# Off-by-one softmax attention and a squared-ReLU feed-forward layer: reordering the opening of a fused kernel, with squares on GpSimd

## The chip, the cores and the metric

The kernel runs on one core of one Trainium2 chip. The metric is device time in microseconds of one execution. A core has TensorE (PE, matrix products, with weight loads shown as PEld), VectorE (DVE), ScalarE (ACT), GpSimd (POOL) and SyncE (SP), which work through their own instruction queues in order and wait for each other by semaphores; data moves between the memory of the device and the core through DMA queues, issued here by SP, ACT and POOL.

## The reference

Inputs are q, k and v of shape (8 batches, 12 heads, 448 positions, 64), and two weights, `w_in` (768 x 2048) and `w_out` (2048 x 768), all float32.

```python
scores = (q @ k.T) / 8
m = max(scores, axis=-1)
e = exp(scores - m)
attn = e / (sum(e) + exp(-m) + 1e-9)
x = (attn @ v), heads put side by side   # (8*448, 768)
h = x @ w_in
out = (max(h, 0) ** 2) @ w_out           # (3584, 768)
```

Multiplying numerator and denominator of `attn` by exp(m) gives exp(scores) / (1 + sum of exp(scores)), up to the 1e-9; the kernel computes this, without the maximum.

## The kernel before

**Tiling.** Two heads form a pair (6 pairs a batch), and a unit is one pair with a stretch of queries. Batch 0 is cut in two by queries: units 0 to 5 are its six pairs with the first 192 queries, units 6 to 11 the same pairs with the last 256. From unit 12 on a unit is one pair with all 448 queries; units 12 to 17 are batch 1, and so on to batch 7. The keys of a unit are taken in 4 chunks of 112, two chunks in each of two *score visits*.

**One unit.** `scores(u, et, c)` is score visit c: TensorE multiplies keys by queries into PSUM (L187 for batches 0 to 2, L199 after) and ScalarE takes the exponential into `et` (L167), one exponential a visit in batch 0 and two from batch 1 on. PSUM has two score buffers. `add_chunks` adds the four chunks of `et` on VectorE (L212, L214 with 448 queries, L216, L219 with fewer), down to a tile `es`. `row_sums` multiplies `es` by a column of ones on TensorE (L248), which sums over partitions, and ScalarE makes the reciprocal as exp(-ln(sum + 1)) (L251, L252, tile `rcp`). `values` multiplies `et` by v on TensorE (L234), and `normalise` multiplies by the reciprocal on VectorE into `xt` (L260, L263), the transposed input of the feed-forward layer.

**The feed-forward layer.** `tile_in` makes one tile of h: TensorE products (called by `product`, L284; in two column halves of 64 that are two matmul instructions, one product), the ReLU on VectorE into `rt` (L301), the square on VectorE into the ring `gs` (L303). A product is one 128-block of `w_in` (16 blocks of 128 columns) with one of six 128-row chunks of `xt`. `tile_out` multiplies `gs` by `w_out` (L330; L286 at the end) and scales into `ot`, which SP stores.

**Order.** There is no scheduler: the order of the instructions on each engine is the order in which this program records them. `queue(t0, n)` puts the `tile_in` tiles of n tokens from t0 into a list, and `drain(ns)` takes products from the list until about `ns` nanoseconds of TensorE work are recorded. Hand-set shares of that work fill TensorE between the attention steps. `run` takes whole tiles.

- Batch 0 and the first queries are transposed by TensorE: `cast` makes float16 (L146 on ScalarE for the first k, L148 on VectorE), `transposes` turns (L156) and VectorE copies to `qk` (L162). Batches 1 and 2 go the same way from float16 loads (`load_natural`). From batch 3 on the DMA transposes (`stage`, `transposed_loads`).
- `keep_warm` records matmuls on zeros that nobody reads, to keep TensorE running in the opening.
- The first loop (`for i in range(2 * NPAIR)`) is batch 0. At unit 6 the list gets the first projection of the first 192 tokens, and units 7 to 11 drain it.
- The second loop is batch 1. In each unit: score visit 0, transposes, drain, score visit 1, row sums and values of the unit before, drain, the adds of this unit, the normalise of the unit before. Row sums of unit i-1 come after score visit 1 of unit i.
- After that comes a loop over pairs of units from batch 2 on (`rows` drains `tile_out`). In its first block the list's leftovers run, and the row sums and values of unit 17 are done.
- Tiles in PSUM come from pools: two score buffers (`s_psum`), three buffers `mp` for transposes, feed-forward tiles, row sums and warm matmuls, and one `xp` for values. A tile that needs a buffer waits until the engine that reads the older one has finished with it.
- GpSimd (POOL) issues the loads that convert to float16, in the order of the program.

Of the kernel before, what the change touches and what calls it, by code (L numbers as in the profile page):

```python
# [15 lines left out]
def kernel(  # L16
# [9 lines left out]
    nc = tc.nc  # L26

    B, H, S, D = q.shape
# [22 lines left out]
    e_pool = ctx.enter_context(tc.tile_pool(name="e", bufs=4))  # L51
    es_pool = ctx.enter_context(tc.tile_pool(name="es", bufs=2))
    z_pool = ctx.enter_context(tc.tile_pool(name="z", bufs=2))
    r_pool = ctx.enter_context(tc.tile_pool(name="r", bufs=2))
    osb_pool = ctx.enter_context(tc.tile_pool(name="osb", bufs=2))

    s_psum = ctx.enter_context(tc.tile_pool(name="s_psum", bufs=2, space=bass.MemoryType.PSUM))
# [19 lines left out]
    def load_v(b, p0, p1):  # L77
        hs = slice(2 * p0, 2 * p1)
        if b not in vns:
            vns[b] = v_pool.tile([P, H, RUN, D], FP16, name="vn")  # L80
        nc.gpsimd.dma_start(out=vns[b][:, hs], in_=v_r[b, :, hs])

    def load_natural(b, p0, p1):

        raw = b == 0 and p1 <= 3
        for n, r in (("q", q_r), ("k", k_r)):
            src = r[b, :, 2 * p0:2 * p1]
            if raw:
                if p0 == 0:
                    whole[n] = e_pool.tile([P, RUN * S], FP32, name="et")  # L90
                t = whole[n][:, p0 * 512:(p0 + 1) * 512].rearrange("p (h t d) -> p h t d", h=2, t=RUN)
                (nc.sync if n == "q" else nc.scalar).dma_start(out=t, in_=src)
            else:
                if p0 % 3 == 0:
                    whole[n] = nat.tile([P, NPAIR, RUN, D], FP16, name=f"{n}n{p0 // 3}")
                t = whole[n][:, 2 * (p0 % 3):2 * (p0 % 3 + p1 - p0)]
                nc.gpsimd.dma_start(out=t, in_=src)
            for pr in range(p0, p1):
                naturals[n, b, pr] = t[:, 2 * (pr - p0):2 * (pr - p0) + 2]
# [42 lines left out]
    def cast(b, pr):  # L142
        for name in "qk":
            f = flat.tile([P, 2, RUN, D], FP16, name=f"flat{name}")
            if b == 0 and pr == 0 and name == "k":
                nc.scalar.activation(out=f, in_=naturals[name, b, pr], func=AF.Copy)  # L146
            else:
                nc.vector.tensor_copy(f, naturals[name, b, pr])  # L148
            naturals[name, b, pr] = f

    def transposes(b, pr):
        tp = mp_tile(FP16)
        for i, name in enumerate("qk"):
            for s in range(RUN):
                for h in range(2):
                    nc.tensor.transpose(tp[64 * h:64 * h + 64, i, P * s:P * s + P],  # L156
                                        naturals[name, b, pr][:, h, s, :], ident[0:P, 0:P])
        if b not in qks:
            qks[b] = qk_pool.tile([128, 3, COLS], FP16, name="qk")
        parts = (0, S // 2, S) if b == 0 and pr == 0 else (0, S)  # L160
        for x, y in zip(parts, parts[1:]):
            nc.vector.tensor_copy(qks[b][:, 0:2, pr * S + x:pr * S + y], tp[:, :, x:y])  # L162

# [111 lines left out]

    FULL, COLS2, ROWS2 = range(3)
    mode = [FULL]
    ots = {}

    def product(out_, lhsT, rhs, start, stop):  # L280
# [7 lines left out]
    def tile_in(t0, n, f0, per):  # L288

        xt, x0 = xts[t0 // S], t0 % S  # L290
        m = per * n
        hp = mp_tile()
        for j in range(per):
            fb = f0 + j
            for dc in range(DCH):
                product(hp[:, j * n:(j + 1) * n], win[:, dc, fb * 128:(fb + 1) * 128],
                        xt[:, dc, x0:x0 + n], start=(dc == 0), stop=(dc == DCH - 1))
                if j < per - 1 or dc < DCH - 1:
                    yield n / 2.4
        rt = r_pool.tile([128, 512], FP16, name="rt")  # L300
        nc.vector.tensor_scalar(out=rt[:, 0:m], in0=hp[:, 0:m], scalar1=0.0, scalar2=None, op0=ALU.max)  # L301
        r = rt[:, 0:m].rearrange("p (j n) -> p j n", j=per)
        nc.vector.tensor_mul(gs[:, f0:f0 + per, t0 % RING:t0 % RING + n], r, r)  # L303
        yield n / 2.4

    def store(c, ot, n0, n1):
# [48 lines left out]
    for pr in range(3):  # L355
        load_natural(0, pr, pr + 1)
    nc.scalar.preload_act_table_set("natural_log_exp_and_others")
    load_v(0, 0, 3)
    ident = consts.tile([128, 128], FP16)
    make_identity(nc, ident)  # L360
    load_natural(0, 3, 4)
    load_natural(0, 4, 6)
    load_v(0, 3, 6)
# [9 lines left out]
    ins, outs = [], []  # L373
    groups = [0]

    def queue(t0, n):

        per = max(1, 512 // n)
        for f0 in range(0, NFFB, per):
            ns = per * DCH * n / 2.4  # L380
            ins.append([ns, ns, tile_in(t0, n, f0, per)])

# [33 lines left out]

    transpose_at = {pr - 1: (0, pr) for pr in range(1, NPAIR)}
    for pr in range(NPAIR):
        transpose_at[NPAIR + 3 + pr] = (1, pr)
    transpose_at[16], transpose_at[17] = (2, 0), (2, 1)  # L420

    def keep_warm(n):
        wp = m_psum.tile([128, 512], FP32, name="mp")
        for _ in range(n):
            nc.tensor.matmul(wp, warm[:, 0:128], warm, start=True, stop=True)
# [18 lines left out]
    keep_warm(9)  # L444
    cast(0, 0)
    transposes(0, 0)
    keep_warm(3)
    cast(0, 1)


    for i in range(2 * NPAIR):
        u, et, es, half = begin(i)
        two = units[i - 2:i] if i and i % 2 == 0 else None
        if i % 2:
            xp = x_psum.tile([128, 512], FP32, name="xp")
        mode[0] = COLS2
        scores(u, et, 0)
        if i == 0:
            keep_warm(4)
        if i == NPAIR:  # L460
            values(units[i - 1], ets.pop(i - 1), xp, units[i - 1][3])
            rcp = row_sums(two, (ess.pop(i - 2)[0:1], ess.pop(i - 1)[0:1]))
            normalise(two, xp, rcp)
            queue(0, FIRST)
            share[0] = left() / (NPAIR + 2)
        if i in transpose_at:
            transposes(*transpose_at[i])
        if i == 0:
            cast(0, 2)
        if i > NPAIR:  # L470
            drain(share[0] * 0.45)
        scores(u, et, 1)
        if 0 < i < NPAIR:
            keep_warm(1)
        if i and i != NPAIR:
            if two and i < NPAIR:
                rcp = row_sums(two, (ess.pop(i - 2)[0:1], ess.pop(i - 1)[0:1]))
            values(units[i - 1], ets.pop(i - 1), xp, (i - 1) % 2 * units[i - 1][3])
            if two and i > NPAIR:
                rcp = row_sums(two, (ess.pop(i - 2)[0:1], ess.pop(i - 1)[0:1]))  # L480
        if i > NPAIR:
            drain(share[0] * 0.3)
        add_chunks(u, et, es, half, 1)
        if two and i != NPAIR:
            normalise(two, xp, rcp)
        add_chunks(u, et, es, half, 2)
        if i > NPAIR:
            drain(share[0] * 0.25)
        if i == NPAIR + 5:
            load_natural(2, 0, 3)  # L490
            for j in range(2):
                load_wout(0, j, 2)


    for i in range(2 * NPAIR, 3 * NPAIR):
        u, et, es, half = begin(i)
        prev = units[i - 1]
        first = i == 2 * NPAIR
        if not first:
            xp = x_psum.tile([128, 512], FP32, name="xp")  # L500
        mode[0] = COLS2
        scores(u, et, 0)
        if i in transpose_at:
            transposes(*transpose_at[i])
        if i == 2 * NPAIR + 2:
            load_natural(2, 3, 6)
            for j in range(2):
                load_wout(HALF, j, 2)
            load_v(2, 0, 6)
            stage(3)  # L510
        drain(left() * 0.5 if first else share[0] * 0.45)
        scores(u, et, 1)
        if first:
            done = units[i - 2:i]
            values(prev, ets.pop(i - 1), xp, prev[3])
            rcp = row_sums(done, (ess.pop(i - 2)[0:1], ess.pop(i - 1)[0:1]))
        else:
            done = [prev]
            rcp = row_sums(done, (ess.pop(i - 1)[0:1],))
            values(prev, ets.pop(i - 1), xp)  # L520
        drain(share[0] * 0.15)
        for step in range(3):
            add_chunks(u, et, es, half, step)
            drain(share[0] * (0.15, 0.1, 0.15)[step])
        if i == 3 * NPAIR - 1 and ins and ins[0][0] < ins[0][1]:
            run(ins)
        normalise(done, xp, rcp)
        if first:
            queue(FIRST, S - FIRST)
            share[0] = left() / (NPAIR + 1.5)  # L530

# [11 lines left out]
    for c in range((NU - 3 * NPAIR) // 2):  # L545
# [16 lines left out]
        add_chunks(ub, eb, sb, hb, 0)  # L562
        mode[0] = COLS2
        for at in pending:
            if at not in rcps:
                rcps[at] = row_sums([units[at]], (ess.pop(at)[0:1],))
            xp = mp_tile()
            values(units[at], ets.pop(at), xp)
            normalise([units[at]], xp, rcps.pop(at))
# [63 lines left out]
```

## Time and profile before

| | |
|---|---|
| time, median of 3 runs | 417.61 us (417.56 to 418.26) |
| span of the profiled execution | 415.9 us |
| instructions | 10695 |
| TensorE busy | 405.5 us (98%) |
| VectorE busy | 278.8 us (67%) |
| ScalarE busy | 238.4 us (57%) |
| GpSimd busy | 36.4 us (9%) |
| granted TensorE clock | full speed |
| start of unit 12 (first score matmul) | 37.23 us |
| start of unit 18, batch 2 (first score matmul) | 67.35 us |

An engine's busy time in a window says how full its queue is there. A wait is read as "engine and line that waited <- engine and line that released it". Matmul ends are modelled and overlap with the next matmul's start, so durations of TensorE work are best taken from start to start. In a timeline row, the columns are start, length, engine, line, operation, output <- inputs, tile, number merged, and in brackets the idle time before it.

### The profile page before, as it was taken

The numbers are of one execution on the slowest core, as the hardware profiler recorded it, in microseconds if no ns is written. First come the engines' busy times: TensorE is split into PE (matmuls) and PEld (weight loads), VectorE is DVE, ScalarE is ACT, GpSimd is POOL, SyncE is SP. The second block draws the span as 40 slices with busy tenths as digits, with TensorE's granted clock in tenths as the row PEclk, the third lists the DMA queues.
The fourth block names the chain that finished last, engine by engine and source line by source line (L and its number), as shares of the span: only waits on it lengthen the run. The fifth ranks groups of instructions, "written<-read, shape, count | busy, mean of one in ns | idle before, by whom it ended". The sixth has DMA issues, their size and how long they took to land.

```text
span 415.9 us, 10695 instructions
## 1 busy us (share of the span) xinstructions
PE 405.5 (98%) x4721; PEld 256.7 (62%) x4721; DVE 278.8 (67%) x535; ACT 238.4 (57%) x329; POOL 36.4 (9%) x58
## 2 busy tenths in 40 slices
PE   8889999899999999999999999999999999999997
PEld 3567666566566666665666666665666666555664
DVE  4769888768865868568766769658676669287000
ACT  4897998664675664673576564674666655100111
POOL 7523220020000200002000400001000000000000
PEclk9999999999999999999999999999999999999999
DMA  9999999889109790199509871198101101010222
GB/s 201 197 197 198 200 197 223 159 120 199 40 2 182 139 192 6 44 199 191 123 2 164 167 151 37 39 186 154 46 2 39 39 2 39 39 39 0 77 76 77
DMA packets 75823, 45.58 MB, mean 110 GB/s; under 512 B 42560, under 2 KB 72000, under 8 KB 75456
## 3 DMA queue, kind: packets, MB, share of 16 engines
q0 software_dynamic: 28848, 22.16, 35.0%
q1 hardware_dynamic: 46208, 22.05, 23.3%
q8 instruction: 37, 0.61, 0.6%
q10 hardware_dynamic: 720, 0.69, 0.6%
q14 instruction: 10, 0.08, 0.1%
HBM read 45.69 MB, written 17.93 MB: 153 GB/s over the span
## 4 chain that ended last, share of the span: by engine, by line
PE 86%; DMA 9%; ACT 2%; DVE 2%; issue 1%; POOL 0%; POOLq 0%
PE mp L284 23%; PE mp L330 17%; PE mp L286 11%; PE xp L284 8%; PE sp L199 6%; PE xp L330 6%; PE mp L234 5%; DMA kn<-in_k_dram 4%; PE xp L286 3%; DMA win<-in_moe_w_in_dram 3%; PE xp L234 3%; PE sp L187 2%; DMA vn<-in_v_dram 2%; PE mp L248 2%; ACT et L167 1%
## 5 line engine op out<-in xcount | busy, mean ns | idle before, releaser
L167 ACT ACTIVATE et<-sp 112x896 f16<-112x896 f32 (+2 forms) x192 | 165.8, 914 | 55.6 <-PE sp L199 40.1
L284 PEld LDWEIGHTS <-win 128*64 128x64 f16 x1536 | 85.3, 110 | 45.7 <-issue 2.8
L284 PE MATMUL mp<-xt,win 128*64 128x448 f16 (+2 forms) x1236 | 110.2, 324 | 1.5 <-DVE xt L263 0.8
L330 PE MATMUL mp<-wout,gs 64*128 64x384 f16 x864 | 102.3, 322 | 0.0
L330 PEld LDWEIGHTS <-gs 64*128 64x128 f16 x1152 | 56.1, 94 | 31.7
L301 DVE TENSOR_SCALAR rt<-mp 128x448 f16<-128x448 f32 (+2 forms) x99 | 61.6, 622 | 17.4 <-PE mp L284 13.3
L303 DVE TENSOR_TENSOR gs<-rt 128x448 f16<-128x448 f16 (+2 forms) x128 | 50.2, 392 | 4.4
L330 PE MATMUL xp<-wout,gs 64*128 64x384 f16 x288 | 52.6, 322 | 0.0
L251 ACT ACTIVATE rcp<-mp,one_b 128x448 f32<-128x448 f32 (+2 forms) x40 | 25.1, 629 | 40.1 <-PE mp L248 35.8
L212 DVE TENSOR_TENSOR es<-et 112x896 f16<-112x896 f16 x42 | 26.0, 620 | 17.7 <-ACT et L167 17.6
L339 ACT ACTIVATE ot<-mp 128x384 f32<-128x384 f32 (+1 forms) x29 | 14.1, 487 | 36.2 <-PE mp L286 27.6
L199 PE MATMUL sp<-qk 64*112 64x224 f16 x480 | 33.8, 260 | 0.0
L286 PEld LDWEIGHTS <-gs 128*128 128x128 f16 x256 | 24.4, 98 | 15.1 <-issue 0.4
L284 PE MATMUL xp<-xt,win 128*64 128x448 f16 x300 | 32.6, 352 | 0.0
L199 PEld LDWEIGHTS <-qk 64*112 64x112 f16 x480 | 26.3, 128 | 9.7 <-issue 5.4
L234 PEld LDWEIGHTS <-vn 112*64 112x64 f16 x432 | 22.1, 109 | 15.3 <-issue 5.2
L286 PE MATMUL mp<-wout,gs 128*128 128x384 f16 (+1 forms) x192 | 31.0, 322 | 0.0
L341 DVE SCALAR_TENSOR_TENSOR ot<-mp,ot 128x384 f32<-128x384 f32 x27 | 15.1, 558 | 21.7 <-PE sp L199 11.6
L252 ACT ACTIVATE rcp<-rcp 128x448 f32<-128x448 f32 (+2 forms) x48 | 27.7, 577 | 1.5
L214 DVE TENSOR_TENSOR es<-es,half 112x896 f16<-112x896 f16 x42 | 26.2, 625 | 1.4
L212 DVE TENSOR_TENSOR half<-et 112x896 f16<-112x896 f16 x42 | 25.9, 616 | 0.3 <-ACT et L167 0.3
L301 DVE TENSOR_SCALAR rt<-xp 128x448 f16<-128x448 f32 x29 | 18.0, 622 | 12.0 <-PE xp L286 8.3
(61 smaller groups left out, 313.9 us busy)
## 6 DMA issues: line engine op xcount, KB each, us to landing
vn<-in_v_dram POOLq DMA_DIRECT2D x7, 672.0 KB, 9.0
out_dram<-ot SPq DMA_DIRECT2D x9, 384.0 KB, 2.8
win<-in_moe_w_in_dram POOLq DMA_DIRECT2D x8, 384.0 KB, 13.9
wout<-in_moe_w_out_dram POOLq DMA_DIRECT2D x4, 768.0 KB, 12.8
stage_q<-in_q_dram POOLq DMA_DIRECT2D x4, 676.0 KB, 10.9
stage_k<-in_k_dram POOLq DMA_DIRECT2D x4, 676.0 KB, 13.3
out_dram<-ot SPq DMA_DIRECT2D x8, 288.0 KB, 3.2
out_dram<-ot SPq DMA_DIRECT2D x9, 192.0 KB, 2.7
```

The lines of the kernel that those rows point to most:

```text
L167: nc.scalar.activation(out=out_, in_=in_, func=AF.Exp, scale=scale)
L199: nc.tensor.matmul(sp[:, odd, h * (S // 2):(h + 1) * (S // 2)], qk[r, which, kx:kx + 2 * P - 1:2], qk[r, 0, x:x + S // 2], start=True, sto ...
L212: nc.vector.tensor_add((es, half[:, 0:2 * S])[step], e[:, 2 * step], e[:, 2 * step + 1])
L214: nc.vector.tensor_add(es, es, half[:, 0:2 * S])
L234: nc.tensor.matmul(xp[64 * h:64 * h + 64, o:o + n], vns[b][:, 2 * pr + h, kk, :], of_head(chunk(et, u, kk // 2, kk), u, h), start=(kk == 0 ...
L251: nc.scalar.activation(out=rcp[:, 0:m], in_=zp[:, 0:m], func=AF.Ln, bias=one_b)
L252: nc.scalar.activation(out=rcp[:, 0:m], in_=rcp[:, 0:m], func=AF.Exp, scale=-1.0)
L284: nc.tensor.matmul(out_[x:x + 64], lhsT[:, x:x + 64], rhs, start=start, stop=stop)
L286: nc.tensor.matmul(out_, lhsT, rhs, start=start, stop=stop)
L301: nc.vector.tensor_scalar(out=rt[:, 0:m], in0=hp[:, 0:m], scalar1=0.0, scalar2=None, op0=ALU.max)
L303: nc.vector.tensor_mul(gs[:, f0:f0 + per, t0 % RING:t0 % RING + n], r, r)
L330: nc.tensor.matmul(o[:, 0:w], g[x:x + 64], wout[x:x + 64, fb, n0:n0 + w], start=(fb == 0), stop=(fb == NFFB - 1))
```

## The change

The change reorders the opening (batches 0 and 1) and moves some work between engines. It is meant to give each engine its work with less waiting on the others.

- Batch 0: both score visits of unit 0 are recorded together; the k cast of pair 1 goes to ScalarE; the copy of pair 1's transposes is split in two; fewer warm matmuls early, some new ones at unit 6; values of units 2 and 4 are recorded one unit later, behind the next unit's scores.
- The first projection of batch 0: only blocks 0 to 11 are queued for the first 192 tokens; blocks 12 to 15 are queued at unit 12 for all 448 tokens together, and blocks 0 to 11 of the last 256 tokens after that. The share of units 7 to 11 is set to 720 ns.
- Batch 1: of a unit's adds only the first is recorded in its own unit; the other two (`finish_sums`) and the row sums and values come in the next unit, ahead of that unit's second score visit. Drains get fixed amounts. All of batch 0's first projection is done before batch 2, as are the sums of unit 17.
- The squares of tiles finished in units 12 to 16 are done by GpSimd; `rt` gets a third buffer.
- Loads: the first v load comes after the identity, all of `w_out` is issued at unit 11, and q, k, v of batch 2 and the staging of batch 3 at unit 16. Transposes of batch 1's last three pairs come one unit later.

```diff
-    r_pool = ctx.enter_context(tc.tile_pool(name="r", bufs=2))
+    r_pool = ctx.enter_context(tc.tile_pool(name="r", bufs=3))
...
-            if b == 0 and pr == 0 and name == "k":
+            if b == 0 and pr < 2 and name == "k":
                 nc.scalar.activation(out=f, in_=naturals[name, b, pr], func=AF.Copy)
...
-        parts = (0, S // 2, S) if b == 0 and pr == 0 else (0, S)
+        parts = (0, S // 2, S) if b == 0 and pr < 2 else (0, S)
...
+    squares = [nc.vector]
...
-        nc.vector.tensor_mul(gs[:, f0:f0 + per, t0 % RING:t0 % RING + n], r, r)
+        squares[0].tensor_mul(gs[:, f0:f0 + per, t0 % RING:t0 % RING + n], r, r)
...
-    load_v(0, 0, 3)
     ident = consts.tile([128, 128], FP16)
     make_identity(nc, ident)
+    load_v(0, 0, 3)
...
-    def queue(t0, n):
+    def queue(t0, n, lo=0, hi=NFFB):
...
-        for f0 in range(0, NFFB, per):
+        for f0 in range(lo, hi, per):
...
-        transpose_at[NPAIR + 3 + pr] = (1, pr)
+        transpose_at[NPAIR + 3 + pr + pr // 3] = (1, pr)
...
+    ALONE = 12
...
-    keep_warm(3)
+    keep_warm(1)
     cast(0, 1)
...
         scores(u, et, 0)
         if i == 0:
-            keep_warm(4)
+            scores(u, et, 1)
+            keep_warm(2)
+        if two and i in (4, NPAIR):
+            values(two[0], ets.pop(i - 2), xp)
         if i == NPAIR:
             values(units[i - 1], ets.pop(i - 1), xp, units[i - 1][3])
+            keep_warm(2)
             rcp = row_sums(two, (ess.pop(i - 2)[0:1], ess.pop(i - 1)[0:1]))
             normalise(two, xp, rcp)
-            queue(0, FIRST)
-            share[0] = left() / (NPAIR + 2)
+            queue(0, FIRST, 0, ALONE)
+            share[0] = 720
...
-        scores(u, et, 1)
+        if i:
+            scores(u, et, 1)
+        if i == NPAIR:
+            keep_warm(3)
...
-            values(units[i - 1], ets.pop(i - 1), xp, (i - 1) % 2 * units[i - 1][3])
+            if i not in (3, 5):
+                values(units[i - 1], ets.pop(i - 1), xp, (i - 1) % 2 * units[i - 1][3])
...
-            for j in range(2):
-                load_wout(0, j, 2)
+            for n0 in (0, HALF):
+                for j in range(2):
+                    load_wout(n0, j, 2)
...
+    def finish_sums(at):
+        for step in (1, 2):
+            add_chunks(units[at], ets[at], *ess[at], step)
+
+    squares[0] = nc.gpsimd
     for i in range(2 * NPAIR, 3 * NPAIR):
...
         scores(u, et, 0)
+        if not first:
+            finish_sums(i - 1)
         if i in transpose_at:
             transposes(*transpose_at[i])
-        if i == 2 * NPAIR + 2:
+        drain(1000 if first else 900 if i in transpose_at else 1300)
+        done = units[i - 2:i] if first else units[i - 1:i]
+        rcp = row_sums(done, [ess.pop(units.index(d))[0:1] for d in done])
+        values(units[i - 1], ets.pop(i - 1), xp, units[i - 1][3] if first else 0)
+        scores(u, et, 1)
+        add_chunks(u, et, es, half, 0)
+        if first:
+            drain(left())
+            normalise(done, xp, rcp)
+            queue(0, S, ALONE, NFFB)
+            queue(FIRST, S - FIRST, 0, ALONE)
+            drain(300)
+        else:
+            drain(600)
+            normalise(done, xp, rcp)
+            drain(850)
+        if i == 2 * NPAIR + 4:
             load_natural(2, 3, 6)
-            for j in range(2):
-                load_wout(HALF, j, 2)
-            load_v(2, 0, 6)
+            load_v(2, 0, NPAIR)
             stage(3)
-        drain(left() * 0.5 if first else share[0] * 0.45)
-        scores(u, et, 1)
-        if first:
-            done = units[i - 2:i]
-            values(prev, ets.pop(i - 1), xp, prev[3])
-            rcp = row_sums(done, (ess.pop(i - 2)[0:1], ess.pop(i - 1)[0:1]))
-        else:
-            done = [prev]
-            rcp = row_sums(done, (ess.pop(i - 1)[0:1],))
-            values(prev, ets.pop(i - 1), xp)
-        drain(share[0] * 0.15)
-        for step in range(3):
-            add_chunks(u, et, es, half, step)
-            drain(share[0] * (0.15, 0.1, 0.15)[step])
-        if i == 3 * NPAIR - 1 and ins and ins[0][0] < ins[0][1]:
-            run(ins)
-        normalise(done, xp, rcp)
-        if first:
-            queue(FIRST, S - FIRST)
-            share[0] = left() / (NPAIR + 1.5)
+            squares[0] = nc.vector
+    drain(left() - 600)
+    finish_sums(3 * NPAIR - 1)
+    run(ins, len(ins))
+    rcps[3 * NPAIR - 1] = row_sums(units[3 * NPAIR - 1:3 * NPAIR], (ess.pop(3 * NPAIR - 1)[0:1],))
...
         for at in pending:
-            if at not in rcps:
-                rcps[at] = row_sums([units[at]], (ess.pop(at)[0:1],))
             xp = mp_tile()
```

## The prediction

> **What bounds the kernel now.** I read the page's slices first, then windows by stage, then the waits of ScalarE in the opening, then the order of time on TensorE and ScalarE in one unit of batch 1. Busy time of the whole run and of the stages (columns: window, its length, then busy us of each engine with its instructions, TensorE clock, DMA share, GB/s):
>
> ```profile
> PE 405.5 (98%) x4721; PEld 256.7 (62%) x4721; DVE 278.8 (67%) x535; ACT 238.4 (57%) x329; POOL 36.4 (9%) x58
> ```
> ```profile
> 9.20:37.20 28.00, 25.46 (x443) 18.20 (x443) 21.51 (x45) 25.20 (x33) 10.81 (x14) 1.00 1.45 197
> 37.20:67.30 30.10, 28.17 (x423) 19.60 (x420) 25.77 (x50) 27.06 (x36) 6.72 (x9) 1.00 1.39 203
> 67.30:83.20 15.90, 14.71 (x191) 9.60 (x190) 11.87 (x22) 10.69 (x15) 0.00 (x0) 1.00 0.89 180
> 83.20:416.00 332.80, 329.69 (x3616) 206.29 (x3616) 216.41 (x411) 172.35 (x242) 12.05 (x22) 1.00 0.43 88
> ```
> After 83.2 us TensorE is the bound (329.7 of 332.8 us) and the change leaves that work as it is, so whatever is won or lost by 83.2 us is carried to the end. Before 83.2 us TensorE and ScalarE are both near full: in batch 0 (9 to 37 us) ScalarE 25.2 of 28.0, in batch 1 (37 to 67 us) TensorE 28.2, ScalarE 27.1 and VectorE 25.8 of 30.1. All that can be won is the slack in this opening.
>
> ```profile
> ACT et L167 <- PE sp L187: 8.0, 16, 1.5
> ```
> That is ScalarE's wait for scores from 5 to 68 us: 8.0 us in 16 waits. One unit of batch 1 (unit 16), TensorE and then ScalarE:
>
> ```profile
> 57.34 0.58 PE L187 MATMUL sp<-qk 64*112 64x448 f16 x4
> 57.86 0.39 PE L156 MATMUL mp<-ident,qn 112*64 112x112 f16 x8
> 58.08 0.36 PE L156 MATMUL mp<-ident,kn 112*64 112x112 f16 x8
> 58.27 0.93 PE L284 MATMUL mp<-xt,win 128*64 128x256 f16 x14
> 59.14 0.81 PE L187 MATMUL sp<-qk 64*112 64x448 f16 x4
> 59.88 0.38 PE L248 MATMUL mp<-es,ones 112*64 112x448 f16 x2
> 60.09 0.92 PE L234 MATMUL xp<-et,vn 112*64 112x448 f16 x8
> 60.85 1.37 PE L284 MATMUL mp<-xt,win 128*64 128x256 f16 x22
> 62.15 0.59 PE L187 MATMUL sp<-qk 64*112 64x448 f16 x4
> ```
> ```profile
> 57.78 3.52 ACT L167 ACTIVATE et<-sp 112x896 f16<-112x896 f32 x4 [0.34 <-PE sp L187]
> 61.19 0.64 ACT L251 ACTIVATE rcp<-mp,one_b 128x448 f32<-128x448 f32 x1
> 61.85 0.58 ACT L252 ACTIVATE rcp<-rcp 128x448 f32<-128x448 f32 x1
> ```
> A unit takes 62.15 - 57.34 = 4.81 us, and ScalarE works 4.65 to 4.75 us of it. TensorE's second score visit took 59.88 - 59.14 = 0.74 us where the first took 0.52, so it stands waiting on ScalarE: ScalarE is the bound of batch 1 and TensorE has some 0.3 us a unit to spare.
>
> **What the Trainium skill says.** GPSIMD Engine Reference, "Elementwise — side-by-side cycle accounting": a two-input operation costs 2.6 cycles an element at 1.2 GHz. SBUF — State Buffer, "Who interferes with whom": a VectorE instruction with two SBUF inputs and a GpSimd instruction that reads SBUF exclude each other for their whole length. Perfetto Trace Analysis, "GPSIMD Engine Instruction": spans of GpSimd in a profile are unreliable. This trace has no elementwise work on GpSimd, so it neither agrees nor disagrees.
>
> **The change part by part.** Times below are start to start in the trace of before.
>
> 1. *Opening (to 12 us).* The k cast of pair 1 (0.41 us on VectorE at 7.22) goes to ScalarE, which idles there; it can start only when k lands (issue at 1.22 plus 5.2 us is 6.4) and ends about 7.0, when the first exp starts anyway (7.03). The second exp follows at 7.8 instead of 8.82, and ScalarE then waits again, for unit 1, which needs transposes and copies. VectorE's chain to unit 2 gets shorter only by the cast less what the split copy adds: I count 0.2 to 0.25 us. Moving a v load behind the identity costs nothing: its consumer at 10.8 us comes after the landing (9.2 plus some 0.6).
>
> 2. *Units 6 to 11.* The share falls from 960 to 720 ns a unit, and the last four blocks of batch 0's first projection are left for later: some 10 products of 192 columns fewer in units 7 to 11. One costs 0.10 us (14 matmuls, two a product, in 0.70 us). TensorE binds there (2.97, 3.46 and 2.94 us for units 9 to 11, ScalarE some 2.6), so 1.0 us is won. With the 0.25 and some 0.15 from values moved behind scores, unit 12's first exp comes at 36.3, not 37.67: 1.4 ahead.
>
> 3. *Unit 12.* Its two score visits had 17 products and a transpose between them and ScalarE waited 1.10 us. Now a transpose less (0.45 us) lies there and the reciprocal (1.25 us) fits the gap. Unit 13's first exp: 36.3 + 4 x 0.86 + 1.25 = 41.0 against 43.37: 2.4 ahead. The k whose landing held TensorE at 38.38 is now needed at 41, and v (25.75 + 16.1 = 41.85) at 42.5: just in time.
>
> 4. *Units 13 to 16, the bill.* Deferred products come here. By the drains a unit holds: score visits 2 x 0.52, transposes 0.41, row sums 0.21, values 0.76, and 14 products of 448 columns at 0.19 (6 took 1.14 us at 92.31), or 8 of these and 9 of 256 columns at 0.118 (11 took 1.30 us), or 23 of the latter. Sums: 5.08, 5.00, 5.14, 5.14; mean 5.09 against 4.81. The added order also makes a ring: row sums of unit i-1 now stand ahead of the second score visit, and the built program makes them wait for the two adds of unit i-1 and the copy behind these. Row sums 0.21, to ScalarE 0.2, reciprocal 1.2, two exps 1.7, adds 0.65 + 0.55, copy 0.55, semaphores 0.1: 5.16 us a turn. TensorE work and ring agree on 5.1, so 4 x 0.3 = 1.2 is given back: 1.2 ahead at unit 17's first exp (61.4).
>
> 5. *End of unit 17, a new wait.* In the built order the row sums of unit 17 stand behind only 8 products (0.95 us) after its last score visit, and ahead of unit 18's scores. From 61.2: 2 x 0.52 + 0.41 + 9 x 0.118 + 0.21 + 0.76 puts the end of the visit at 64.7; its exps end at 66.25, two adds at 67.5. TensorE stands from 65.65 to 67.55, and the scores of unit 18, reached at 67.35 before, come at 67.8. All queued rows of the output projection wait behind. ScalarE then does the reciprocal (1.2) ahead of unit 18's exps, which stops TensorE another 0.6 at the next visit.
>
> 6. *Batch 2's first block (67.35 to 83.19).* Twelve leftover products (1.42) and waits of 0.46 + 0.36 + 0.15 + 0.22 = 1.19 us around the late reciprocal go; about 0.9 of waits stay, as the second row sums and the next tile need buffers that VectorE's copies free. 15.84 - 1.42 - 1.19 + 0.9 + 0.6 = 14.7 by subtraction; walked through instruction by instruction it is 13.9, because the first tile of batch 1 no longer waits for the reciprocal at all. I take 13.9: 67.8 + 13.9 = 81.7 against 83.19, which is 1.5 us ahead.
>
> 7. *Squares on GpSimd.* Ten squares in units 12 to 16 leave VectorE (0.36 to 0.43 each, some 0.85 us a unit). It had 0.3 us a unit free, so this makes room for the adds. A square of 512 elements costs 512 x 2.6 / 1.2 = 1.1 us by the page's price (an estimate), 0.43 at the least, by the VectorE row. Two a unit are 2.2 of 5.1 us, and three r buffers hold them. Their readers come in batch 2, so their own length costs nothing. What may cost is the exclusion: a unit's last relu ends close to when the adds of the ring start. Bounds: 0, or 0.6 to 1.0 us in each of four units. I take 0 for the forecast and keep 2 to 3.5 for the range, because whichever starts first wins, and the add is often released first.
>
> 8. *The rest.* Output weights issued together in unit 11 bring no more bytes, since the DMA engines are full to 65 us anyway, and they are read after 67 us. The q and k of batch 2 (issued near 62, landing in 6 to 9 us) are needed at 75. Fewer, wider products save 24 x 0.012 = 0.3 us, inside the sums.
>
> Sum: 417.6 - 1.5 = 416.1.
>
> **Rivals.**
> A. *The ring is stretched by the exclusion.* For it: the ring has no slack, and three of four units have a relu within 1 us of the adds. Against: VectorE loses 0.85 us a unit. Time: 4 x 0.7 = 2.8 us back, 418.9: slower.
> B. *Both engines overlap better than my sums.* If units 13 to 16 keep 4.81 us (1.1) and the stand at unit 17 shrinks by half (1.0), 416.1 - 2.1 = 414.0. For it: ScalarE's own work is only 4.7 us a unit, and VectorE gets emptier. Against: TensorE's 5.09 us of work are counted from rows.
> C. *It cancels:* a collision in two units (1.3 us): 417.4, no change.
>
> **How the numbers follow.** Forecast 0.45, A 0.27, B 0.16, C 0.12. The forecast (0.36% below) lies beyond 0.2% (0.84 us) with a margin of only 0.7 us, so a few hundredths of its chance go to no change: faster 0.58, same 0.14, slower 0.28. The range reaches to B's and A's times: 413.8 to 419.0.
>
> **What would show it.** Unit 13's first exp near 41.0 (step 3). Units 13 to 16 at 5.1 us a turn, with the row sums waiting for VectorE's copy (4). A TensorE wait of nearly 2 us for the row sums of unit 17 (5). No reciprocal wait and no 256-column products in batch 2's first block (6). VectorE adds of 0.62 us that stay 0.62, or grow beside squares of about 1.1 us (7). I am wrong if the adds of the ring grow, if v lands after its reader, or if unit 17's row sums don't wait.

## The result, and the profile after

The changed kernel takes 421.94 us (median; 421.48 to 422.50) against 417.59 for the kernel before on the same chip: ratio 1.0102, 95% interval 1.0083 to 1.0121. It is slower by 4.3 us; forecast was 416.1, and 419.0 was the upper end of the range. The profiled span grew by 4.8 us, from 415.9 to 420.7; about 0.9 us of this is a drop of the clock, which two of the four executions have, the profiled one among them.

Busy time by stage in the changed kernel (columns as in the prediction; the same windows). From the ReLU and the products on, its lines are numbered one higher than before: L284 is now L285, L301 L302, L303 L304, L330 L331.

```profile
9.20:37.20 28.00, 25.68 (x428) 17.51 (x428) 20.95 (x44) 24.50 (x33) 11.14 (x14) 1.00 1.45 197
37.20:67.30 30.10, 27.04 (x384) 17.70 (x383) 23.71 (x39) 24.35 (x32) 15.33 (x16) 1.00 1.02 152
67.30:83.20 15.90, 13.35 (x156) 7.82 (x157) 9.00 (x17) 11.19 (x15) 2.48 (x4) 0.89 1.09 179
```
In the first window TensorE is idle for 2.32 us (before: 2.54). In the second it is idle for 3.06 (1.93 before) and ScalarE, which was near full, has lost 2.7 us of work. In the third TensorE is idle for 2.55 (1.19), and its granted clock fell to 0.89. What ends TensorE's waits between 38 and 90 us says where; before, the longest of them was 0.5 us:

```profile
PE mp L248 <- DVE qk L162: 2.9, 5, 0.8
PE mp L248 <- DVE es L214: 2.5, 1, 2.5
PE sp L187 <- ACT et L167: 0.9, 2, 0.5
```
L248 is the row sums: five waits for VectorE's copy of transposes (four in units 14 to 17, 2.2 us, and one in batch 2), and one of 2.5 us for its adds.

**The ring.** One turn in the changed kernel, unit 15 to 16, of all engines in order of time:

```profile
55.35 0.38 PE L248 MATMUL mp<-es,ones 112*64 112x448 f16 x2 [0.48 <-DVE qk L162]
...
55.77 0.63 ACT L251 ACTIVATE rcp<-mp,one_b 128x448 f32<-128x448 f32 x1 [0.82 <-PE mp L248]
...
56.44 0.58 ACT L252 ACTIVATE rcp<-rcp 128x448 f32<-128x448 f32 x1
56.92 1.71 ACT L167 ACTIVATE et<-sp 112x896 f16<-112x896 f32 x2
...
57.90 0.69 DVE L302 TENSOR_SCALAR rt<-mp 128x512 f16<-128x512 f32 x1 [1.46 <-PE mp L285]
58.51 0.61 DVE L260 TENSOR_TENSOR xt<-xp,rcp 128x448 f16<-128x448 f32 x1
...
58.67 1.04 POOL L304 TENSOR_TENSOR gs<-rt 128x512 f16<-128x512 f16 x1 [1.34 <-DVE rt L302]
...
59.04 1.15 DVE L212 TENSOR_TENSOR half<-et 112x896 f16<-112x896 f16 x1
...
60.22 0.62 DVE L214 TENSOR_TENSOR es<-es,half 112x896 f16<-112x896 f16 x1
60.76 0.62 DVE L162 COPY qk<-mp 128x896 f16<-128x896 f16 x1
...
61.43 0.38 PE L248 MATMUL mp<-es,ones 112*64 112x448 f16 x2 [0.76 <-DVE qk L162]
```
Read it as a relay: row sums, reciprocal, the second pair of exps, add, add, copy, next row sums. A turn is 61.43 - 55.35 = 6.08 us. The exps end at 58.63, but the add starts at 59.04, behind a ReLU and a normalise in VectorE's queue. Beside the square on GpSimd (58.67 to 59.71) it takes 1.15 us where it took 0.62 before. First exps of units 13 to 17 start at 41.67, 47.53, 53.23, 59.02 and 65.10: 5.86 us a unit against 4.81 (the expectations below say 5.84, from a first start taken as 41.74). VectorE's waits between 38 and 72 us are for TensorE and ScalarE only: GpSimd delays it by the stretched adds, and not by holding the `rt` buffers.

**The stand.** TensorE after unit 17's last score visit:

```profile
68.40 0.59 PE L187 MATMUL sp<-qk 64*112 64x448 f16 x4
68.92 1.06 PE L285 MATMUL mp<-xt,win 128*64 128x256 f16 x16
72.50 0.51 PE L248 MATMUL mp<-es,ones 112*64 112x448 f16 x2 [2.51 <-DVE es L214]
72.94 0.99 PE L187 MATMUL sp<-qk 64*112 64x448 f16 x4
73.72 3.09 PE L331 MATMUL mp<-wout,gs 64*128 64x384 f16 x22
```
The same place in the kernel before:

```profile
67.35 0.58 PE L187 MATMUL sp<-qk 64*112 64x448 f16 x4
67.77 1.95 PE L330 MATMUL mp<-wout,gs 64*128 64x384 f16 x22
69.56 0.54 PE L187 MATMUL sp<-qk 64*112 64x448 f16 x4
```
Unit 18's scores stand behind the waiting row sums and start at 72.94 (before: 67.35); with the row sums out of their way they start at 69.92 (run "unit 17's sums later" below). The 22 matmuls after them took 76.65 - 73.72 = 2.93 us; the same 22 took 69.56 - 67.77 = 1.79 before. That is the clock, not a wait: the profile gives it as half there (shown in the last section).

### The profile page after: what moved, and what is told of

Same layout as the page of the kernel before. It is cut to its first block, busy times and chain, and to the rows that moved or that the text cites. A ratio compares the mean times of both kernels' runs of the same rounds, so it can differ in the third digit from the quotient of the medians.

```text
span 420.7 us, 10614 instructions
## 1 busy us (share of the span) xinstructions
PE 406.5 (97%) x4674; PEld 254.4 (60%) x4674; DVE 277.2 (66%) x525; ACT 238.7 (57%) x330; POOL 47.9 (11%) x68
## 4 chain that ended last, share of the span: by engine, by line
PE 88%; DVE 6%; ACT 4%; issue 1%; DMA 1%; DVEq 0%
PE mp L285 24%; PE mp L331 17%; PE mp L287 10%; PE xp L285 7%; PE sp L199 6%; PE xp L331 6%; PE mp L234 5%; PE xp L287 4%; PE xp L234 3%; PE sp L187 3%; ACT et L167 2%; PE mp L248 2%; DVE qk L162 1%; DVE half L212 1%; DMA et<-in_q_dram 1%
## 5 line engine op out<-in xcount | busy, mean ns | idle before, releaser
L285 PE MATMUL mp<-xt,win 128*64 128x448 f16 (+2 forms) x1212 | 111.7, 331 | 0.2 <-DVE qk L162 0.2
L285 PEld LDWEIGHTS <-win 128*64 128x64 f16 x1488 | 82.4, 110 | 46.7 <-issue 3.3
L331 PE MATMUL mp<-wout,gs 64*128 64x384 f16 x864 | 103.5, 326 | 0.0
L302 DVE TENSOR_SCALAR rt<-mp 128x448 f16<-128x448 f32 (+2 forms) x101 | 62.8, 622 | 27.4 <-PE mp L285 15.2
L331 PEld LDWEIGHTS <-gs 64*128 64x128 f16 x1152 | 56.5, 95 | 32.7 <-issue 1.6
L331 PE MATMUL xp<-wout,gs 64*128 64x384 f16 x288 | 52.6, 322 | 0.0
L304 DVE TENSOR_TENSOR gs<-rt 128x448 f16<-128x448 f16 (+2 forms) x118 | 46.2, 392 | 4.0
L340 ACT ACTIVATE ot<-mp 128x384 f32<-128x384 f32 (+2 forms) x29 | 13.9, 480 | 55.3 <-PE mp L287 44.2
L251 ACT ACTIVATE rcp<-mp,one_b 128x448 f32<-128x448 f32 (+2 forms) x38 | 23.8, 627 | 37.5 <-PE mp L248 37.5
L285 PE MATMUL xp<-xt,win 128*64 128x448 f16 x276 | 30.0, 352 | 0.0
L287 PE MATMUL mp<-wout,gs 128*128 128x384 f16 (+2 forms) x192 | 29.6, 313 | 0.0
L214 DVE TENSOR_TENSOR es<-es,half 112x896 f16<-112x896 f16 x42 | 27.6, 657 | 1.4
L187 PE MATMUL sp<-qk 64*112 64x448 f16 (+2 forms) x192 | 23.6, 324 | 3.4 <-ACT et L167 2.7
```

Of the source, the lines that this page charges most:

```text
L187: nc.tensor.matmul(sp[:, h, o:o + n], qk[r, 1, x + P * kk:x + P * kk + P], qk[r, 0, x + q0:x + q0 + n], start=True, stop=True)
L214: nc.vector.tensor_add(es, es, half[:, 0:2 * S])
L285: nc.tensor.matmul(out_[x:x + 64], lhsT[:, x:x + 64], rhs, start=start, stop=stop)
L287: nc.tensor.matmul(out_, lhsT, rhs, start=start, stop=stop)
L304: squares[0].tensor_mul(gs[:, f0:f0 + per, t0 % RING:t0 % RING + n], r, r)
L331: nc.tensor.matmul(o[:, 0:w], g[x:x + 64], wout[x:x + 64, fb, n0:n0 + w], start=(fb == 0), stop=(fb == NFFB - 1))
```

## The experiments

Two theories stood at the start. The first: GpSimd's squares stretch the adds of the ring, and that is the main loss. The second: the new order itself, ring and stand, is the loss, whichever engine squares. Times are medians; each ratio is to the kernel before on the same chip (417.7 to 417.9 us there). "Gain" is against the changed kernel's 421.94, across chips on which the kernel before differs by 0.1 to 0.3 us. Some runs have executions with the drop of the clock (mean clock 0.996) and some without (0.999 or 1.0), which moves a median by up to 0.9 us. So where a gain is small, the text compares executions of the same clock: the changed kernel has 421.48 and 421.55 without the drop (421.5), 422.33 and 422.50 with it (422.4).

| run | us | ratio (95%) | gain |
|---|---|---|---|
| squares on VectorE | 421.09 | 1.0074 (1.0056 to 1.0091) | 0.85 |
| warm matmuls in the stand | 421.54 | 1.0086 (1.0071 to 1.0101) | 0.4 |
| unit 17's sums later | 419.57 | 1.0038 (1.0023 to 1.0053) | 2.37 |
| before + opening | 417.64 | 0.9995 (0.9987 to 1.0004) | |
| second visit first | 421.07 | 1.0083 (1.0070 to 1.0095) | 0.87 |
| before + GpSimd squares | 418.23 | 1.0008 (0.9999 to 1.0016) | |
| new batch 0, old batch 1 and loads | 418.18 | 1.0009 (1.0001 to 1.0017) | 3.76 |
| three edits | 418.44 | 1.0013 (1.0006 to 1.0019) | 3.50 |
| copy off the ring | 421.69 | 1.0094 (1.0080 to 1.0108) | 0.25 |
| normalise behind | 423.36 | 1.0138 (1.0123 to 1.0154) | -1.42 |
| both of these, sums later | 420.09 | 1.0054 (1.0041 to 1.0067) | 1.85 |
| before + early sums | 417.07 | 0.9983 (0.9977 to 0.9990) | |
| no squares (part missing) | 420.06 | 1.0052 (1.0040 to 1.0065) | 1.88 |
| reciprocal behind | 423.80 | 1.0139 (1.0125 to 1.0153) | -1.86 |
| before + opening + early sums | 417.17 | 0.9983 (0.9977 to 0.9990) | |
| no squares (part missing), sums later | 417.18 | 0.9986 (0.9979 to 0.9992) | 4.76 |
| before + sums ahead of visit | 421.40 | 1.0087 (1.0073 to 1.0101) | |

### The stand and the clock

Unit 17's row sums go into batch 2's first block:

```diff
-    rcps[3 * NPAIR - 1] = row_sums(units[3 * NPAIR - 1:3 * NPAIR], (ess.pop(3 * NPAIR - 1)[0:1],))
...
         rows(11)
+        if c == 0:
+            rcps[i - 1] = row_sums([units[i - 1]], (ess.pop(i - 1)[0:1],))
         scores(ua, ea, 1)
```


> The changed kernel with the row sums of unit 17 recorded behind the first 11 products of the output projection in batch 2, instead of in front of unit 18's scores. Theory 1 (the stand of 2.5 us and the low clock after it are lost outright): both go, 421.9 - 2.5 - 1.7 = about 417.7. Theory 2 (the stand only moves, since the exps of batch 2 wait for the reciprocal or the tile of batch 1 waits for unit 17): 420.5 to 421.9.

2.37 us won, 1.95 against the executions without the drop: the stand is one large part of the loss, and another remains.

Warm matmuls ahead of the same row sums keep TensorE's clock up:

```diff
     run(ins, len(ins))
+    keep_warm(11)
     rcps[3 * NPAIR - 1] = row_sums(units[3 * NPAIR - 1:3 * NPAIR], (ess.pop(3 * NPAIR - 1)[0:1],))
```


> The changed kernel with 11 matmuls on zeros (2.35 us) in front of unit 17's row sums, where TensorE stood for 2.5 us; nothing useful is added. Theory 1 (the stand lowers the granted TensorE clock: the 22 matmuls after it took 2.93 us instead of 1.79, and the scores and row sums before them some 0.5 us more): the clock stays full and the time falls by 1.5 to 1.7 us, to about 420.3. Theory 2 (the slow matmuls have another cause, such as output weights landing late): no change, 421.9.

Only 0.4 us came, and the single executions say why. With the stand filled none of the four has the drop, and they take 421.45 to 421.68, as the changed kernel does without it. So the drop costs 0.9 us when it happens, in half of the executions, and nothing else was won. The size expected took it for a cost of every execution.

### The squares

Back on VectorE:

```diff
-    squares[0] = nc.gpsimd
```


> The changed kernel with its ten squares of units 12 to 16 back on VectorE; all else as changed. Theory 1 (exclusion: GpSimd squares hold VectorE's adds, seen as adds of 1.04 to 1.34 us instead of 0.62 in four units, 2.3 us in sum): units 13 to 16 fall from 5.84 to about 5.3 us each and the time from 421.9 to about 419.7. Theory 2 (the order alone makes the loss: row sums ahead of the second score visit close a ring without slack): VectorE's squares lie in the same ring, so units stay at 5.8 or more, and the time at 421.9 or above.

All adds are 0.62 us again, but only 0.85 us is won (0.8 to 1.05 at the same clock), as VectorE's own square (0.39 to 0.43) now stands ahead of the adds of the ring: the cost was exchanged. The row sums still wait 1.9 us for VectorE's copy. The same squares on GpSimd in the kernel before:

```diff
+    squares[0] = nc.gpsimd
     for i in range(2 * NPAIR, 3 * NPAIR):
```


> The kernel before with one part alone: squares of units 12 to 16 on GpSimd, three r buffers. The exclusion of adds and squares takes place here too (adds of 1.0 to 1.3 us where they meet). If it costs by itself, some 0.5 us a unit are lost: 419.5 to 420. If it costs only inside the ring, which the kernel before doesn't have (a unit's sums are needed a whole unit later), nothing changes: 417.4 to 417.9.

Adds of this run, 40 to 68 us (count, then busy us and mean ns; before, these two groups have 625 and 617 ns):

```profile
L214 DVE TENSOR_TENSOR es<-es,half 112x896 f16<-112x896 f16 x6 | 5.7, 950 | 0.2
L212 DVE TENSOR_TENSOR es<-et 112x896 f16<-112x896 f16 x6 | 4.9, 823 | 0.2 <-ACT et L167 0.2
```
They stretched by (5.7 - 3.8) + (4.9 - 3.7) = 3.1 us, and the time grew by 0.4 with an interval that reaches zero. The third group, `half`, kept its 619 ns. Exclusion costs little where nobody waits for the adds. To price it inside the ring, the squares were left out:

```diff
+        if squares[0] is nc.gpsimd:
+            nc.vector.tensor_scalar(out=gsx, in0=hp[:, 0:m].rearrange("p (j n) -> p j n", j=per), scalar1=0.0, scalar2=None, op0=ALU.max)
+        else:
...
```


> The changed kernel with the squares of units 12 to 16 left out (the relu writes its result where the square would go, so this part of the computation is missing), on neither GpSimd nor VectorE. If the stretched adds (2.3 us more over four units) lie in the ring, units 13 to 16 fall from 5.84 to about 5.3 us, 2.0 us won beside the stand that stays: 419.9. If another link (TensorE's deferred products at 5.15, the normalise ahead of the adds) takes over at once: 421 to 421.5.

The same stretch of VectorE as in the ring above, now without squares:

```profile
57.51 0.61 DVE L260 TENSOR_TENSOR xt<-xp,rcp 128x448 f16<-128x448 f32 x1
58.03 0.61 DVE L212 TENSOR_TENSOR half<-et 112x896 f16<-112x896 f16 x1
58.68 0.62 DVE L214 TENSOR_TENSOR es<-es,half 112x896 f16<-112x896 f16 x1
```
The units take 5.86, 5.11, 5.30 and 5.47 us, mean 5.43, and 1.88 us is won, as expected. In batch 1 the row sums now wait 0.15 us in all for VectorE's copy, where it was 2.2. Between executions of the same mean clock the gain is 2.4 us (at 1.0, one execution) and 2.2 (at 0.996).

With both suspects gone:

> The changed kernel with the squares of units 12 to 16 left out (this part of the computation is missing) and unit 17's row sums inside batch 2's first block. If exclusion and stand are the whole loss and add: 421.94 less 1.9 less 2.35 is 417.7, the time of the kernel before although ten squares are missing, because the products postponed from units 7 to 11 are repaid in full. If there is more to win once both are gone (the 1.6 us ahead at unit 13 kept): 416.5. If they overlap: 418.5 or more.

417.18: they add. At the same clock, without the drop, 2.4 for the squares and 1.95 for the stand are 4.35, and 421.5 - 417.18 is 4.3. So the two are the whole loss against the kernel before. Even so, and with ten squares missing, it is only 0.6 us faster than that kernel: the change has hardly a gain of its own to set against them.

### The order of batch 1

Units 0 to 11 as changed, batch 1 in the old order (adds in their own unit, second visit first, late sums of unit 17, squares on VectorE; batch 2's loads at unit 14, and drains by share, as before):

> The changed kernel's opening and units 6 to 11 (with the four blocks left for later), then batch 1 in the order of the kernel before: second score visit first, adds in their own unit, sums of unit 17 late in batch 2's first block, squares on VectorE. If the order of batch 1 is what loses the time, the 1.6 us won by unit 13 are kept but for the deferred products (units at 4.9 to 5.1, 4 x 0.2): 416.8. If the deferred products themselves fill TensorE and cost what they saved, no change against the kernel before or worse: 417.6 to 419.

418.18, so what was changed from unit 12 on (order, squares, drains and loads together; this run doesn't part them) accounts for 3.76 of the 4.1 to 4.3 us. But the 1.6 us ahead at unit 13 are gone by batch 2: unit 17's first exp is at 61.95 (before: 62.59) and unit 18's at 68.33 (67.78). The units take 5.04 us instead of 4.81, and 1.2 us more are lost from unit 17 to unit 18. TensorE runs the products postponed from units 7 to 11 in these two places (ahead of unit 18's scores stand 40 product matmuls, 22 before), so the lead they gave was repaid.

Only the visit's place changed:

```diff
+        if not first:
+            scores(u, et, 1)
         rcp = row_sums(done, [ess.pop(units.index(d))[0:1] for d in done])
         values(units[i - 1], ets.pop(i - 1), xp, units[i - 1][3] if first else 0)
-        scores(u, et, 1)
+        if first:
+            scores(u, et, 1)
```


> The changed kernel, but in units 13 to 17 the second score visit is put ahead of the row sums and values again; adds stay a unit later, squares stay on GpSimd. If the ring (row sums, reciprocal, second pair of exps, adds, copy, row sums) sets the 5.84 us a unit, units 13 to 16 fall to what TensorE's own work needs, 5.1 to 5.2 us: 4 x 0.65 = 2.6 us won, 419.3; the stand ahead of unit 17's row sums stays. If TensorE's work or the exclusion of the adds by the squares sets the pace, the order of the two makes no difference: 421.5 to 422.

A miss: 0.87 us, 0.5 to 0.7 at the same clock. The row sums still wait, 2.8 us in four waits (three in batch 1, 2.2 us), because adds a unit later stand behind a normalise that waits for a reciprocal behind two exps. The reverse edit, sums and values ahead of the visit in the kernel before:

> The kernel before with the order of the ring alone: in units 13 to 17 row sums and values ahead of the second score visit; adds stay in their own unit, squares on VectorE. If the ring needs the adds a unit later to close, the row sums find their adds done long before and ScalarE only swaps reciprocal and exps: 417.6 to 418.2. If sums ahead of the visit cost by themselves (exps of the second visit 1.2 us later, adds and copies behind them): 419 or more.

Also a miss, and the most telling one: 3.7 us slower, with adds in their own unit and no GpSimd. TensorE's waits between 38 and 90 us in it:

```profile
PE mp L248 <- DVE qk L162: 2.4, 3, 1.2
PE xp L234 <- DVE xt L260: 1.4, 3, 0.6
```
Either part, sums earlier (this run) or adds later (the run before it), leaves row sums waiting for VectorE's queue. Three edits together (visit first, later sums of unit 17, squares on VectorE):

> The changed kernel with three edits at once: second score visit ahead of row sums (no ring), unit 17's row sums inside batch 2's first block, squares on VectorE. If ring, stand and exclusion are the whole loss and add up: 421.9 less 2.6 (ring), 2.35 (stand, measured) and 0.3 is 416.6, below the kernel before. If they overlap (a delay taken from one lets another bind, ScalarE above all): about 418.5.

418.44, which is what later sums and squares on VectorE account for (at a mean clock of 1.0: 1.95 and 1.05 us off 421.5): if these two add, which no run tested without the visit, the visit's place brought nothing measurable.

### Links of the ring

Transposes behind the values (copy off the ring); the normalise behind the next adds and copy; these two with the later sums; and the reciprocal behind the second visit's exps, with the late normalise:

> The changed kernel with the transposes of units 13 to 15 recorded behind the row sums and values, so that the row sums wait for the two adds alone and not for the copy of the transposes behind them. If the ring through VectorE's queue sets the pace, each turn loses the copy (0.55 to 0.6 us) in units 13 to 15, 3 x 0.55 = 1.6 us: 420.3. If the wait only moves to another link (a buffer, or the adds' own place in the queue), nothing: 421.5 to 422.

> The changed kernel with the normalise of a unit recorded behind the next unit's adds and copy, so that on VectorE nothing but a relu stands ahead of the adds of the ring. If the adds' late start (0.4 us behind the end of the exps) is a term of the ring, 4 x 0.4 = 1.6 us are won: 420.3. If an earlier start only brings the adds under the GpSimd squares from their beginning, they stretch more and the time stays: 421.5 to 422.

> The changed kernel with three edits: transposes behind row sums, normalise behind the next adds, and unit 17's row sums inside batch 2's first block. If the ring's terms add, units 13 to 16 come down to TensorE's own 5.15 us (0.65 x 4 = 2.6), and with the 2.35 measured for the later sums: 417.0, no better than the kernel before, since postponed products are only repaid. If links of the ring take each other's place: 418.5 to 419.5.

> The changed kernel with the reciprocal of units 12 to 16 behind the second score visit's exps on ScalarE (row sums stay ahead on TensorE) and each normalise behind the next unit's adds and copy. The ring then no longer passes through ScalarE's 1.2 us. If it closed there, row sums stop waiting and units 13 to 16 come to TensorE's own 5.15 us: 4 x 0.65 = 2.6 won, 419.3. If the adds and the copy alone are too late for row sums ahead of the second visit, the units stay at 5.6 or more: 421 or above.

The gain that each hoped for did not come. Without the copy 0.7 us is won at the same clock (421.69, all four executions with the drop, against 422.4), half of what was expected: the row sums wait for the add instead (4.3 us in five waits, the stand's 2.5 among them), and the transposes now delay the second visit. With the normalise out of the way the add starts at once, and the square then meets the second add (1.24 to 1.35 us), while values wait for their buffer: 1.3 to 1.5 us slower. Both edits with the later sums are 0.5 us slower than the later sums alone (419.57). Without ScalarE's 1.2 us the row sums wait as long as before (2.9 us in five waits), and the time is that of the late normalise alone: without the drop 422.79, against 422.71 and 422.86. Several paths of nearly the same length run between two row sums; cutting one leaves the others. How much each contributes was not settled.

### The opening, and a kernel that beats both

> The kernel before with only the opening's part of the change: both score visits of unit 0 together, the k cast of pair 1 on ScalarE, split copy, v load behind the identity, warm matmuls as changed, values of units 2 and 4 a unit later. Theory 1 (the opening brings little, since unit 12's first exp of the changed kernel was only 0.48 us ahead): 417.2 to 417.6. Theory 2 (the opening brings 0.5 us or more and it was the share of units 7 to 11 that brought nothing): 416.8 to 417.1. Slower than before would say that values and warm matmuls ahead of unit 5's row sums cost more than the opening wins.

> The kernel before with one edit: unit 17's row sums and reciprocal in batch 2's first block, ahead of the second score visit, instead of at its end. If the waits around the late reciprocal (0.46 for its buffer, 0.2 and 0.15 around it) are time, 0.5 us are won: 417.3. If ScalarE's 1.2 us ahead of the exps makes TensorE wait at the next score visit as in the changed kernel, it is taken back: 417.7 to 418.3.

> The kernel before with the opening parts of the change and with unit 17's sums early in batch 2's first block. If the two add: 417.07 less 0.2 is 416.9. If the opening's 0.1 to 0.2 us are lost in the waits for scores of units 1 to 5: 417.1.

The opening alone does nothing that can be measured. The kernel before with unit 17's sums ahead of the second visit of batch 2's first block takes 417.07 us: faster by 0.17% (0.10 to 0.23), the fastest here. Its TensorE waits between 67 and 84 us, where the kernel before waited 0.5 for the reciprocal, 0.4 for the copy and 0.2 for the ReLU:

```profile
PE sp L187 <- ACT et L167: 0.4, 1, 0.4
PE mp L284 <- DVE rt L301: 0.2, 1, 0.2
```
The reciprocal's wait is gone; ScalarE's later exps take back 0.4. Adding the opening gives 417.17, the same.

## Why the prediction was wrong

The lead over the kernel before, where the prediction gives it, and as the profiled execution has it:

| point | forecast | measured |
|---|---|---|
| unit 12, first exp | 1.4 ahead | 0.48 ahead |
| unit 13, first exp | 2.4 ahead | 1.70 ahead |
| unit 17, first exp | 1.2 ahead | 2.51 behind |
| unit 18, first scores | 0.45 behind | 5.59 behind |
| unit 20, first scores | 1.5 ahead | 4.84 behind |

So of 6.3 us, 0.7 are missing by unit 13, 3.0 in units 13 to 16, 1.4 at the end of unit 17 and 1.2 in batch 2's first block.

- **Step 1, opening.** 0.2 to 0.25 us predicted by unit 2; 0.12 measured (first exp at 11.55, not 11.67), and nothing in the time alone.
- **Step 2, units 6 to 11.** Unit 12's first exp was forecast at 36.3; it came at 37.19. ScalarE waited for scores here too (0.44 us ahead of unit 12), so taking products off TensorE did not move the visits forward one for one.
- **Step 3, unit 12.** The reciprocal did fit the gap: 1.2 us gained, 1.0 forecast.
- **Step 4, units 13 to 16: a mis-sized term.** The ring was named with its right links and its wait (row sums for VectorE's copy), but at 5.16 us a turn. The units took 5.86. In the turn shown the sum lacked 0.41 us (the add starts behind ReLU and normalise) and 0.53 (stretched add), together 0.94; the turn exceeded the sum by 6.08 - 5.16 = 0.92. Bill: 4 x (5.86 - 4.81) = 4.2 us, not 1.2.
- **Step 5, the stand.** A TensorE wait of 1.9 us was forecast, 2.51 came. Its mechanism was right, its price too small: from unit 17's first exp to unit 18's scores the lead was to fall by 1.65 us, and it fell by 3.08. Of the 1.4 more, 0.6 is the wait of the ring's last row sums for the copy (behind an add of 1.34 us), 0.6 the ReLU and the square of VectorE's queue ahead of the last adds, and 0.2 the slower row sums at half clock.
- **Step 6, batch 2's first block.** 13.9 us by the walk, 14.7 by subtraction; 87.95 - 72.94 = 15.0 measured. The fallen clock, which no step had, is 0.9 of this: with warm matmuls in the stand the block takes 86.94 - 72.81 = 14.1, near the walk.
- **Step 7, the exclusion: the step that failed.** It took 0 out of "0, or 0.6 to 1.0 us in each of four units", since the add "is often released first". In all four turns an add met a square that had started first, and grew by 0.62, 0.42, 0.53 and 0.72 us: 2.3 of the 3.0 us by which step 4 was short. The ring had no slack to hide it; leaving the squares out won 1.88 us in the medians, 2.2 to 2.4 at the same clock, or 0.5 to 0.6 a unit. Rival A named this and its direction, but its 418.9 is still 3.0 us short, as the other steps missed too. The page SBUF — State Buffer, "Who interferes with whom", was right: adds of 0.62 us took 1.04 to 1.34 beside squares.
- **Step 8.** No cost or gain of the loads shows: between 38 and 90 us TensorE waits for no DMA (before: 0.3 us).

The sum failed in kind as well. TensorE's work is fixed, so only its idle time can be won: 10.4 us of the span before (415.9 - 405.5), 14.2 after (420.7 - 406.5). First exps that come earlier because products were postponed are a loan. Step 4 charged its repayment with 1.2 us and kept a net gain; with the new batch 0 and the old batch 1 none was left (418.18).

## What to carry to other kernels

Budget the idle time of the engine that bounds the whole, not how far ahead some stage starts: postponed work is repaid. A wait put at the head of an in-order queue costs everything queued behind it, so put row sums where much ready work is ahead of them; and where a loop over several engines has no slack, count every instruction that stands ahead of a link in each queue, and take a possible collision at its bound, not at zero.

## What the hardware showed unexpectedly

**The clock drop is a matter of chance.** In the profiled execution it is at half for 3.4 us (columns: window, length, busy time of PE, PEld, DVE, ACT, POOL, clock, DMA share, GB/s):

```profile
72.00:73.00 1.00, 0.50 (x4) 0.17 (x6) 0.44 (x1) 0.00 (x0) 0.00 (x0) 0.81 1.45 195
73.00:74.00 1.00, 1.00 (x7) 0.49 (x8) 0.00 (x0) 0.92 (x2) 0.00 (x0) 0.50 1.46 199
...
76.00:77.00 1.00, 1.00 (x14) 0.64 (x12) 0.56 (x1) 0.00 (x0) 0.00 (x0) 0.99 0.10 22
```
TensorE: Matmul & The Clock Gate, "What's actually happening", tells of a free-running window of about 3.4 us and of half clock after an idle one. The length agrees: 0.38 + 3 + 0.02 us here, at half clock, and 3.4 in each of the three other profiles that have a drop, which begins 0.1 to 1.5 us after the stand. But a stand of 2.4 to 2.6 us was enough here, in 19 of 30 executions of the seven kernels that have it, and no drop came in those whose stand was filled or moved. In the six of them that also have executions without the drop, these were on average 0.9 to 1.2 us shorter.

**GpSimd squares.** Squares that did not start within an add took 0.83, 0.93 and 1.04 us for 384, 448 and 512 elements, the last a little under the 1.1 us estimated from GPSIMD Engine Reference. Two of 512 back to back (the kernel before with GpSimd squares) took 2.08 us from start to end, so the single spans can be believed here. Where an add and a square overlap, whichever started second is recorded longer by the overlap less 0.13 to 0.15 us, on either engine: in the ring shown the square ends 0.67 us after the add's start, and the add grew by 0.53. A square that began within an add took 1.24 to 1.41 us in the changed kernel, and left the add its 0.62.
